# Matmuls of zeros in TensorE's idle stretches, and a phi softmax by halves of the heads

## The chip, the cores and the metric

The kernel runs on one core of a Trainium2 chip. A core has TensorE (PE) for matmuls, VectorE (DVE), ScalarE (ACT) and GpSimd (POOL) for work on vectors, and SyncE (SP), whose queue issues the DMA transfers. The metric is the device time of one execution in microseconds (us).

## The reference

Per batch `b` and head `h` (8 of each, 576 tokens, 64 features), a softmax over 576 tokens of `phi` (32 memories) pools keys and values; queries attend to the pooled memories; the result goes through a real part of a 2D FFT, a layer norm and a feed-forward block (512 to 2048 to 512).

```python
a = exp(phi - max(phi, axis=2)); a = a / (sum(a, axis=2) + 1e-9)
k_m = einsum('bhsm,bhsd->bhmd', a, k); v_m = einsum('bhsm,bhsd->bhmd', a, v)
attn = softmax(scale * q @ k_m.T)          # over the 32 memories
x = (attn @ v_m).transpose(0, 2, 1, 3).reshape(B, S, H * D)
u = x + real(fft(fft(x, axis=1), axis=2))
un = (u - mean(u)) / sqrt(var(u) + 1e-6)
out = u + relu(un @ w_ch1) @ w_ch2
```

## The kernel before

Heads go in four pairs `g`; both heads of a pair fill 128 partitions. The mixing of a batch, `background()`, is a generator that the feed-forward loop advances, so that mixing of later batches runs beside the feed-forward of earlier ones. For batch 0 there is nothing beside it: this is the head of the program.

- `pooling_weights(b)` transposes phi on PE with an f32 identity (`pf`, and its last 64 tokens in `pl`), takes maxima on DVE, exponentials on ACT. For the batches below `NX = 2` it scales the exponentials on ACT (L311), transposes them back (`pt_e`), and copies them to `et`. Each of the two halves holds two head pairs (`g // 2`).
- `pair_memory` multiplies keys and values with `et` in f32: 10 matmuls with 64 columns for each pair, `pm`, which the trace shows as 20 records. DVE masks them with `mk`, a table that a DMA loads (`kmf`, `vmf`).
- `pair_scores` computes 6 matmuls `psc` (12 records) and a softmax of them, mostly on DVE for batch 0 (L440 to L480).
- `values` (`pv`, the transposes `pt_vbd`), `spectrum` (`pa`), `pair_transpose` (`attnT`) and the tiles of `mix_m` and `mix_x` (`pp_t`, `px_t`) give the sums `u` in `uring`. `norm_chunk` normalizes (L631 to L642) and transposes (`pt_unT`).
- The first chunk of the feed-forward block runs in f32: `ffn1_direct` (`ph`, L675) and `ffn2_direct` (`po`, L692). Meanwhile the weights, 64-bit words in memory, are converted to f32 by ACT (L771) and DVE (L773, L774, L784), and split into two f16 parts (L803 to L808). Later chunks use the f16 parts (`ph` L255, `po` L728).

The program is written in sequence, and a scheduler then sets the order of each engine's queue by a timeline of its own; `tc.issue_after` ties single instructions to others. Each engine takes its instructions in the order of its queue.

Of the kernel before, what the change touches and what calls it, by code (L numbers as in the profile page):

```python
# [10 lines left out]
F32 = mybir.dt.float32  # L11
F16 = mybir.dt.float16
# [39 lines left out]
EB = 14  # L52
# [79 lines left out]
def kernel(  # L132
# [10 lines left out]
    nc = tc.nc  # L143

    const = ctx.enter_context(tc.tile_pool(name="const", bufs=1))
    psg = ctx.enter_context(tc.tile_pool(name="psg", bufs=4, space=PSUM))
    ps1 = ctx.enter_context(tc.tile_pool(name="ps1", bufs=2, space=PSUM))
    ps2 = ctx.enter_context(tc.tile_pool(name="ps2", bufs=2, space=PSUM))
# [3 lines left out]
    phs = const.tile([P, NST, NG, 2 * M], F32, name="phs")  # L152
# [15 lines left out]
    mk = small[:, 0:68]  # L168
# [4 lines left out]
    ic = small[:, 714:715]  # L173
    s1, is1, s2, is2 = (small[:, 716 + i * NW : 716 + (i + 1) * NW] for i in range(4))
    ident = small[:, 768:832].bitcast(F16)
    make_identity(nc, ident)
    identf = const.tile([P, P], F32, name="identf")
    make_identity(nc, identf)
    stg = const.tile([P, 3, 4 * UW], F16, name="stg")
    w1t = const.tile([P, NW + 1, 2, NK, UB * P], F16, name="w1t")  # L180
    w2s = const.tile([P, NF + UB, 2, DM], F16, name="w2s")
    nc.gpsimd.memset(ones, 1.0)
    nc.gpsimd.memset(et.rearrange("p g l t c -> p (g l t c)"), 0.0)
    unring = const.tile([P, 2, 2, CH, NK, P], F16, name="unring")
    uring = const.tile([P, NU, DM], F32, name="uring")
    hring = const.tile([P, NW, 2, 4, P], F16, name="hring")

    nk = 2 * NST * P
# [11 lines left out]
    def tiny(tag, n, bufs=2):  # L200
        if tag not in rings:
            rings[tag] = [taken[0], 0]
            taken[0] += n * bufs
        o, i = rings[tag]
        rings[tag][1] += 1
        o += i % bufs * n
        assert taken[0] <= 400, taken
        return scratch[:, o : o + n]
# [6 lines left out]
        return pt[:, c0 : c0 + n]  # L215

    qi = [0]

    def norm_scale(dst_s, dst_i, sq, n, expo, key):

        t = tiny("p2t", 4, 4)
        nc.vector.tensor_scalar(
            out=t[:, :n].bitcast(I32),
            in0=sq.bitcast(I32),
            scalar1=24,
            scalar2=23,
            op0=ALU.logical_shift_right,
            op1=ALU.logical_shift_left,
        )
        nc.vector.tensor_scalar(  # L230
            out=dst_i, in0=t[:, :n], scalar1=2.0**-104, scalar2=2.0 ** (64 - expo), op0=ALU.max, op1=ALU.mult
        )
        nc.vector.reciprocal(out=dst_s, in_=dst_i)

    def transpose(dst, src, on_pe, key):

# [12 lines left out]
    def groups():  # L249

        last = [None]

        def mm(out, lhsT, rhs, start, stop):
            with tc.issue_after(last[0].ins) if start and last[0] is not None else nullcontext():
                m = nc.tensor.matmul(out, lhsT=lhsT, rhs=rhs, start=start, stop=stop)  # L255
            if stop:
                last[0] = m

        return mm


    def load_phi(b):
        for g in range(NG):
            nc.sync.dma_start(out=phs[:, :, g], in_=raw[b, g, :, KV:KVP].rearrange("p (t c) -> p t c", t=NST))

    def load_pair(b, g):
        r = rawt
        if b == 0 and g > 1:
            r = w2s.rearrange("p a l c -> p (a l c)").bitcast(F32)[:, RKQ * (g - 2) : RKQ * (g - 1)]
        elif g % 2 == 1:  # L270
            r = stg[:, 0].bitcast(F32)
        for part, src in ((r[:, :KV], raw[b, g, :, :KV]), (r[:, KV:], raw[b, g, :, KVP:])):
            with tc.issue_after(marks["q"].ins) if b == 0 and "q" in marks else nullcontext():
                marks["q"] = nc.sync.dma_start(out=part, in_=src)
        return r

    def load_vt():
# [2 lines left out]
        marks["vt"] = nc.sync.dma_start(out=v, in_=vt_d)  # L280
        return [v[:, g * 2 * DM : (g + 1) * 2 * DM] for g in range(NG)]

    def pooling_weights(b):

        pl = psg.tile([P, 512], F32, tag="g", name=f"pl_{b}")
        mx = tiny("mx", 4, 2)
        pf = []
        for g in range(2):
            pf.append(psg.tile([P, 512], F32, tag="g", name=f"pf_{b}_{g}"))
            for t in range(NST):  # L290
                dst = pf[g][:, t * P : (t + 1) * P] if t < 4 else pl[:, g * P : (g + 1) * P]
                nc.tensor.transpose(dst, phs[:, t, 2 * g : 2 * g + 2].rearrange("p g c -> p (g c)"), identf)
            nc.vector.tensor_reduce(out=mx[:, g : g + 1], in_=pf[g], axis=AX.X, op=ALU.max)
        rest = pl[:, : 2 * P].rearrange("p (g s) -> p g s", g=2)[:, :, : S - 4 * P]
        nc.vector.tensor_reduce(out=mx[:, 2:4], in_=rest, axis=AX.X, op=ALU.max)
        nc.vector.tensor_tensor(out=mx[:, 0:2], in0=mx[:, 0:2], in1=mx[:, 2:4], op=ALU.max)
        nc.vector.tensor_scalar(out=mx[:, 0:2], in0=mx[:, 0:2], scalar1=-1.0, scalar2=None, op0=ALU.mult)
        su = tiny("su", 4, 2)
        for g in range(2):
            m = mx[:, g : g + 1]  # L300
            nc.scalar.activation(pht[:, g, : 4 * P], pf[g], AF.Exp, bias=m, accum_out=su[:, g : g + 1])
            nc.scalar.activation(pht[:, g, 4 * P :], rest[:, g], AF.Exp, bias=m, accum_out=su[:, 2 + g : 3 + g])
        nc.vector.tensor_tensor(out=su[:, 0:2], in0=su[:, 0:2], in1=su[:, 2:4], op=ALU.add)
        nc.vector.tensor_scalar(
            out=su[:, 0:2], in0=su[:, 0:2], scalar1=1e-9, scalar2=2.0**-EB, op0=ALU.add, op1=ALU.mult
        )
        nc.vector.reciprocal(out=su[:, 2:4], in_=su[:, 0:2])
        for g in range(2):
            r = su[:, 2 + g : 3 + g]
            if b < NX:  # L310
                nc.scalar.activation(pht[:, g], pht[:, g], AF.Copy, scale=r)  # L311
                pt = psg.tile([P, 512], F32, tag="g", name=f"pt_e{b}_{g}")
                for t in range(4):
                    nc.tensor.transpose(pt[:, t * P : (t + 1) * P], pht[:, g, t * P : (t + 1) * P], identf)
                nc.vector.tensor_copy(out=et32[:, g, :4], in_=pt.rearrange("p (t c) -> p t c", c=P))
                half_t = pl[0 : S - 4 * P, (2 + g) * P : (3 + g) * P]
                nc.tensor.transpose(half_t, pht[:, g, 4 * P :], identf)
                nc.scalar.copy(out=et32[0 : S - 4 * P, g, 4], in_=half_t)
                continue
            nc.scalar.activation(elt[:, 0, :S], pht[:, g], AF.Copy, scale=r)  # L320
            nc.vector.scalar_tensor_tensor(
                out=elt[:, 1, :S], in0=pht[:, g], scalar=r, in1=elt[:, 0, :S], op0=ALU.mult, op1=ALU.subtract
            )
            transpose(
                et[:, g].rearrange("p l t c -> p (l t) c"), elt.rearrange("p l c -> p (l c)"), False, f"et_{b}_{g}"
            )
# [319 lines left out]
    def norm_chunk(c):  # L646

        unT = unring[:, c % 2]
        unT0 = unT.rearrange("p l t k c -> p (l t k c)").bitcast(F32)
        unT0 = unT0.rearrange("p (k t c) -> p k t c", k=NK, t=CH)  # L650
        for i in range(CH):
            idx = CH * c + i
            norm_tile(idx, us[idx], un[:, i])
            if c == 0:
                pt = psg.tile([P, 512], F32, tag="g", name=f"pt_unT_{i}")
                for k in range(NK):
                    nc.tensor.transpose(pt[:, k * P : (k + 1) * P], un[:, i, k * P : (k + 1) * P], identf)
                marks["uh0"] = nc.scalar.copy(out=unT0[:, :, i], in_=pt.rearrange("p (k c) -> p k c", k=NK))
        if c == 0:
            return unT0  # L660
        marks[f"uh{c}"] = nc.scalar.copy(out=ud[:, 0], in_=un)  # L661
        marks[f"ul{c}"] = nc.gpsimd.tensor_tensor(out=ud[:, 1], in0=un, in1=ud[:, 0], op=ALU.subtract)  # L662
        transpose(
            unT.rearrange("p l t k c -> p (l t k) c"), ud.rearrange("p l t c -> p (l t c)"), False, f"unT_{c}"
        )
        return unT
# [181 lines left out]
    marks = {}  # L848
# [6 lines left out]
    def background():  # L855
# [56 lines left out]
        while True:  # L912
            yield n_tiles, 0

    load_phi(0)
    first = [load_pair(0, 0)]
    nc.sync.dma_start(out=mk, in_=mk_d)
    first += [load_pair(0, g) for g in range(1, NG)]
    marks["load"] = marks["q"]
    with tc.issue_after(marks["load"].ins):  # L920
# [29 lines left out]

    while made < 2:
        made, room = next(bg)
    unTs = {0: norm_chunk(0)}
    hs = {c: [] for c in range(n_chunks)}
    po = [ps2.tile([P, 512], F32, tag="o", name=f"po_0_{t}") for t in range(CH)]
# [29 lines left out]
    for n in range(NW, n_steps):  # L985
        c, j = divmod(n, NW)
# [75 lines left out]
```

## Time and profile before

| | us |
|---|---|
| median of 3 runs | 996.77 (996.4 to 997.15) |
| the profiled execution | 996.51 |
| its span | 994.6 |
| PE busy | 955.8 (96% of the span) |
| DVE busy | 568.1 (57%) |
| ACT busy | 456.3 (46%) |
| POOL busy | 228.0 (23%) |

The span goes from the first to the last instruction; 1.9 us of the time lie around it. PE's busy time counts from the start of a matmul to its modelled end, so it does not tell whether the array streams all the time. The page also has a row of the clock that was granted to PE, in tenths of full speed, in 40 slices of 24.9 us. The profile's lines below have, if they are single instructions: start, length, engine, line, operation, tile written <- tiles read, shape, count, and in brackets the idle time before and what ended it.

### The profile page before, as it was taken

How to read it: one execution, taken by the hardware profiler on the slowest of the kernel's cores; microseconds unless marked ns; L12 is line 12 of the kernel's file. 1: busy time of each engine (PE TensorE's matmuls, PEld its weight loads, DVE VectorE, ACT ScalarE, POOL GpSimd, SP SyncE). 2: the span in 40 equal slices, each digit the busy share in tenths (PEclk: the TensorE clock that was granted, in tenths of full speed). 3: DMA queues.
4: the chain of work that ended last, by engine and by line, in shares of the span. 5: the costliest groups of instructions: out<-in, count | busy, mean ns of one | idle time of the engine just before them, and what ended most of it. 6: DMA issues, size and time to landing. Idle time of an engine off the chain costs nothing.

```text
span 994.6 us, 18638 instructions
## 1 busy us (share of the span) xinstructions
PE 955.8 (96%) x7644; PEld 685.8 (69%) x7644; DVE 568.1 (57%) x1287; ACT 456.3 (46%) x913; POOL 228.0 (23%) x249
## 2 busy tenths in 40 slices
PE   5769999899999999999999999999999999999998
PEld 5756678666677777767767767777777777766664
DVE  1689967867655575657532576657745676311111
ACT  2265557586535563655431555456545543411100
POOL 1122235235221241233120032113311241300000
PEclk9979999999999999999999999999999999999999
DMA  9706545064222641384210643164213411210000
GB/s 351 270 1 253 184 152 154 2 138 117 64 43 59 136 98 41 56 153 103 58 22 22 117 120 61 48 119 121 68 43 62 101 19 35 44 39 4 22 22 22
DMA packets 115957, 88.06 MB, mean 89 GB/s; under 512 B 100384, under 2 KB 100384, under 8 KB 113824
## 3 DMA queue, kind: packets, MB, share of 16 engines
q1 hardware_dynamic: 115872, 86.87, 34.6%
q8 instruction: 60, 0.98, 0.4%
q14 instruction: 25, 0.20, 0.1%
HBM read 58.15 MB, written 9.44 MB: 68 GB/s over the span
## 4 chain that ended last, share of the span: by engine, by line
PE 84%; DVE 9%; ACT 2%; DMA 2%; issue 1%; SPq 0%; POOL 0%; DVEq 0%; ACTq 0%; POOLq 0%
PE po L728 34%; PE ph L255 33%; PE pm L255 5%; PE pp_t L255 3%; PE psc L255 2%; PE px_t L255 1%; PE pa L548 1%; PE pv L521 1%; PE po L692 1%; DVE w1t L784 1%; DVE uring L617 1%; DVE w2s L774 1%; DMA et<-elt 1%; DMA uring<-in_w 1%; DMA rawt<-in_raw 1%
## 5 line engine op out<-in xcount | busy, mean ns | idle before, releaser
L255 PE MATMUL ph<-unring,w1t 128*128 128x256 f16 x3264 | 390.3, 273 | 2.4 <-DVE scratch L638 1.4
L728 PE MATMUL po<-w2s,hring 128*128 128x512 f16 x1632 | 381.1, 380 | 3.1 <-ACT w2s L838 1.8
L255 PEld LDWEIGHTS <-w1t 128*128 128x128 f16 x3264 | 316.0, 98 | 66.3 <-issue 2.6
L728 PEld LDWEIGHTS <-hring 128*128 128x128 f16 x1632 | 157.6, 98 | 161.5 <-issue 5.6
L719 DVE SCALAR_TENSOR_TENSOR hring<-ph,hring 128x512 f16<-128x512 f32 x136 | 93.3, 686 | 157.4 <-ACT hring L718 156.9
L718 ACT ACTIVATE hring<-ph 128x512 f16<-128x512 f32 x136 | 80.1, 589 | 167.7 <-PE ph L255 167.6
L456 POOL TENSOR_TENSOR aring<-aring,scratch 128x384 f32<-128x384 f32 x28 | 24.7, 882 | 186.6 <-DVE scratch L454 163.5
L641 POOL TENSOR_TENSOR scratch<-scratch,small 128x1 f32<-128x1 f32 x36 | 23.9, 679 | 165.6 <-DVE scratch L640 152.9
L255 PEld LDWEIGHTS <-stg 128*128 128x128 f16 x1152 | 46.1, 98 | 10.3 <-issue 1.7
L373 POOL TENSOR_TENSOR stg<-rawt,stg 128x640 f16<-128x640 f32 x12 | 17.6, 1464 | 122.4 <-ACT rawt L372 122.4
L662 POOL TENSOR_TENSOR ud<-un,ud 128x1024 f16<-128x1024 f32 x17 | 36.7, 2160 | 33.9 <-ACT ud L661 33.8
L255 PE MATMUL pm<-et,stg 128*128 128x64 f16 (+1 forms) x780 | 39.1, 203 | 2.0 <-DMA et<-elt 2.0
L440 DVE TENSOR_REDUCE scratch<-psc 128x12 f32<-128x384 f32 x32 | 17.8, 556 | 39.2 <-PE psc L255 39.1
L255 PE MATMUL pp_t<-vh,at 128*128 128x255 f16 (+3 forms) x288 | 36.7, 273 | 0.0
L603 DVE SCALAR_TENSOR_TENSOR share<-pp_t,scratch,small 128x257 f32<-128x257 f32 (+1 forms) x48 | 21.0, 479 | 26.6 <-ACT small L600 26.5
L740 DVE SCALAR_TENSOR_TENSOR uring<-po,small,uring 128x512 f32<-128x512 f32 x34 | 24.5, 744 | 19.2 <-PE po L728 19.2
L675 PE MATMUL ph<-unring,w1t 128*128 128x256 f32 x128 | 33.5, 409 | 2.0 <-DVE w1t L784 1.5
L475 ACT CAST aeo<-eo 128x384 f16<-128x384 f32 x30 | 15.3, 510 | 43.9 <-DVE eo L472 43.9
L450 ACT ACTIVATE aring<-aring,scratch 128x384 f32<-128x384 f32 x24 | 14.6, 610 | 45.0 <-DVE aring L449 45.0
L617 DVE SCALAR_TENSOR_TENSOR uring<-px_t,scratch,share 128x256 f32<-128x256 f32 (+1 forms) x80 | 33.9, 476 | 0.2
L692 PE MATMUL po<-w2s,hring 128*128 128x512 f32 x64 | 31.5, 621 | 2.4 <-ACT hring L678 2.4
L675 PEld LDWEIGHTS ph<-unring,w1t 128*128 128x128 f32 x128 | 26.0, 207 | 11.1 <-issue 4.6
(226 smaller groups left out, 1271.9 us busy)
## 6 DMA issues: line engine op xcount, KB each, us to landing
rawt<-in_raw SPq DMA_DIRECT2D x15, 640.0 KB, 5.6
stg<-in_raw SPq DMA_DIRECT2D x15, 640.0 KB, 5.1
out<-uring SPq DMA_DIRECT2D x36, 256.0 KB, 2.1
stg<-in_w SPq DMA_DIRECT2D x7, 1024.0 KB, 5.1
rawt<-in_raw SPq DMA_DIRECT2D x15, 384.0 KB, 3.2
stg<-in_raw SPq DMA_DIRECT2D x15, 384.0 KB, 3.2
phs<-in_raw SPq DMA_DIRECT2D x32, 160.0 KB, 5.2
w2s<-in_w SPq DMA_DIRECT2D x4, 1024.0 KB, 9.6
```

The source lines that it names most:

```text
L255: m = nc.tensor.matmul(out, lhsT=lhsT, rhs=rhs, start=start, stop=stop)
L456: eng.tensor_tensor(out=a, in0=a, in1=sm.unsqueeze(2).to_broadcast([P, 12, M]), op=ALU.mult)
L603: nc.vector.scalar_tensor_tensor(out=tm[rows, w * NJ : (w + 1) * NJ], in0=pp[rows, :NJ], scalar=beta[rows], in1=qs[rows], op0=ALU.mult, op ...
L617: nc.vector.scalar_tensor_tensor(out=u[rows, hs], in0=px[rows, hs], scalar=igx[rows], in1=tm[rows, w * NJ + half : w * NJ + half + 256], o ...
L641: nc.gpsimd.tensor_tensor(out=rs, in0=rs, in1=half, op=ALU.pow)
L662: marks[f"ul{c}"] = nc.gpsimd.tensor_tensor(out=ud[:, 1], in0=un, in1=ud[:, 0], op=ALU.subtract)
L675: nc.tensor.matmul(ph, lhsT=w[:, k, f * P : (f + 1) * P], rhs=unTs[0][:, k], start=(k == 0), stop=(k == NK - 1))
L692: nc.tensor.matmul(po[t], lhsT=h[:, f, t], rhs=w[:, f], start=(j == 0 and f == 0), stop=(j == NW - 1 and f == UB - 1),)
L718: nc.scalar.activation(h[:, 0], phv, AF.Relu)
L719: nc.vector.scalar_tensor_tensor(out=h[:, 1], in0=phv, scalar=0.0, in1=h[:, 0], op0=ALU.max, op1=ALU.subtract)
L728: nc.tensor.matmul(po[t], lhsT=hs[j][:, lh, f * 2 + t], rhs=w2s[:, j * UB + f, lw, :], start=(j == 0 and f == 0 and i == 0), stop=(j == NW ...
L740: nc.vector.scalar_tensor_tensor(out=u, in0=po[t], scalar=cout if c else 0.5, in1=u, op0=ALU.mult, op1=ALU.add)
```

## The change

1. `keep_busy(n)` issues `n` f16 matmuls 128x128 by 128x512 of zeros into a PSUM buffer of the pool `ps2` that nothing reads. The zeros lie in the last slot of `uring`, which DVE clears at the start. `KEEP` has the numbers: 8 ahead of phi, 18 behind phi's transposes, 4 and 3 behind the transposes back of the two halves, 22 ahead of the first norm. `marks["pe"]` ties them behind the matmul that was issued last.
2. For the batches below `NX`, `pooling_f32` replaces the common softmax: maximum, sum and reciprocal are taken for each half by itself, and DVE instead of ACT scales the exponentials (128x576, in place).
3. A small Exp of a single column at the start makes ACT load its table there; the f32 identity is built before the f16 one.
4. The load of `mk` is written ahead of all others.

```diff
+KEEP = [8, 18, 0, 0, 22, 4, 3]
...
-    make_identity(nc, ident)
+    uring = const.tile([P, NU, DM], F32, name="uring")
+    zeros = uring[:, NU - 1].bitcast(F16)[:, :DM]
+    nc.vector.memset(zeros, 0.0)
     identf = const.tile([P, P], F32, name="identf")
     make_identity(nc, identf)
+    make_identity(nc, ident)
+    warm = const.tile([P, 1], F32, name="warm")
+    nc.vector.memset(warm, 0.0)
+    nc.scalar.activation(warm, warm, AF.Exp)
...
+    def keep_busy(n):
+
+        pt = ps2.tile([P, 512], F32, tag="o", name=f"keep_{len(kept)}")
+        kept.append(pt)
+        with tc.issue_after(marks["pe"].ins) if "pe" in marks else nullcontext():
+            for _ in range(n):
+                nc.tensor.matmul(pt, lhsT=zeros[:, :P], rhs=zeros, start=True, stop=True)
...
+    def pooling_f32(b, pl, pf, rest):
+
+        mx, su = tiny("mx", 4, 2), tiny("su", 4, 2)
+        for g in range(2):
+            nc.vector.tensor_reduce(out=mx[:, g : g + 1], in_=pf[g], axis=AX.X, op=ALU.max)
+            nc.vector.tensor_reduce(out=mx[:, 2 + g : 3 + g], in_=rest[:, g], axis=AX.X, op=ALU.max)
+            m = mx[:, g : g + 1]
+            nc.vector.tensor_scalar(
+                out=m, in0=m, scalar1=mx[:, 2 + g : 3 + g], scalar2=-1.0, op0=ALU.max, op1=ALU.mult
+            )
+            nc.scalar.activation(pht[:, g, : 4 * P], pf[g], AF.Exp, bias=m, accum_out=su[:, g : g + 1])
+            nc.scalar.activation(pht[:, g, 4 * P :], rest[:, g], AF.Exp, bias=m, accum_out=su[:, 2 + g : 3 + g])
+        if b == 0:
+            keep_busy(KEEP[1])
+        for g in range(2):
+            t = su[:, g : g + 1]
+            nc.vector.tensor_scalar(
+                out=t, in0=t, scalar1=su[:, 2 + g : 3 + g], scalar2=1e-9, op0=ALU.add, op1=ALU.add
+            )
+            nc.vector.tensor_scalar(out=t, in0=t, scalar1=2.0**-EB, scalar2=None, op0=ALU.mult)
+            nc.vector.reciprocal(out=t, in_=t)
+            nc.vector.tensor_scalar(out=pht[:, g], in0=pht[:, g], scalar1=t, scalar2=None, op0=ALU.mult)
+        for g in range(2):
...
+            marks["pe"] = nc.tensor.transpose(half_t, pht[:, g, 4 * P :], identf)
+            if b == 0:
+                keep_busy(KEEP[5 + g])
+            nc.vector.tensor_copy(out=et32[:, g, :4], in_=pt.rearrange("p (t c) -> p t c", c=P))
+            nc.scalar.copy(out=et32[0 : S - 4 * P, g, 4], in_=half_t)
...
-            if b < NX:
-                nc.scalar.activation(pht[:, g], pht[:, g], AF.Copy, scale=r)
...
+    nc.sync.dma_start(out=mk, in_=mk_d)
     load_phi(0)
+    keep_busy(KEEP[0])
     first = [load_pair(0, 0)]
-    nc.sync.dma_start(out=mk, in_=mk_d)
...
     while made < 2:
         made, room = next(bg)
+    keep_busy(KEEP[4])
     unTs = {0: norm_chunk(0)}
```

PE's queue between the transposes of phi and the first `pm`, before; `pl` takes the last 64 tokens of both directions:

```order
L292 MATMUL pf_1_135<-identf,phs 128x128 x4
L292 MATMUL pl_127<-identf,phs 128x128
L314 MATMUL pt_e_0_153<-identf,phs 128x128 x4
L317 MATMUL pl_127<-identf,phs 64x128
L314 MATMUL pt_e_1_162<-identf,phs 128x128 x4
L255 MATMUL pm_0_170<-et,rawt 128x64 x10
```

The same place now:

```order
L340 MATMUL pf_1_147<-identf,phs 128x128 x4
L340 MATMUL pl_140<-identf,phs 128x128
L248 LDWEIGHTS uring
L248 MATMUL keep_163<-uring 128x512
L323 MATMUL pt_e_0_190<-identf,phs 128x128 x4
L325 MATMUL pl_140<-identf,phs 64x128
L323 MATMUL pt_e_1_203<-identf,phs 128x128 x4
L270 MATMUL pm_0_215<-et,rawt 128x64 x10
```

The pair of `keep` stands here 18 times, and further ones behind both `pl` of the transposes back (4 and 3).

DVE's queue from the last masking of `pm` to the first sums of the scores' softmax, before; the conversion of the first weights stands between the second and the third pair:

```order
L347 TENSOR_TENSOR vmf<-pm_1_183,small 128x128
L773 TENSOR_SCALAR w1t<-w1t 128x1024
L774 SCALAR_TENSOR_TENSOR w1t<-w1t 128x1024
L784 SCALAR_TENSOR_TENSOR w1t<-w1t 128x1024
L346 TENSOR_TENSOR share<-pm_2_196,small 128x64
L347 TENSOR_TENSOR vmf<-pm_2_196,small 128x128
L346 TENSOR_TENSOR share<-pm_3_209,small 128x64
L347 TENSOR_TENSOR vmf<-pm_3_209,small 128x128
L440 TENSOR_REDUCE scratch<-psc_0_222 128x12
```

Now, at the scores:

```order
L389 TENSOR_TENSOR vmf<-pm_3_254,small 128x128
L815 TENSOR_SCALAR w1t<-w1t 128x1024
L482 TENSOR_REDUCE scratch<-psc_0_267 128x12
L816 SCALAR_TENSOR_TENSOR w1t<-w1t 128x1024
L491 TENSOR_TENSOR aring<-psc_0_267,scratch 128x384
L482 TENSOR_REDUCE scratch<-psc_1_291 128x12
L826 SCALAR_TENSOR_TENSOR w1t<-w1t 128x1024
```

The three operations of the conversion moved from among the `pm` to among the scores.

SP's queue from the last load of a head pair on, before; `small` holds the masks, `hring` takes the table `vt`:

```order
L274 DMA w2s<-in_raw 128x768
L922 DMA ct<-in_ct 128x1740
L761 DMA w1t<-in_w 128x2048
L917 DMA small<-in_mk 128x68
L280 DMA hring<-in_vt 128x4096
```

The same place now:

```order
L289 DMA w2s<-in_raw 128x768
L965 DMA ct<-in_ct 128x1740
L957 DMA small<-in_mk 128x68
L803 DMA w1t<-in_w 128x2048
L295 DMA hring<-in_vt 128x4096
```

The load of the masks, written first, stands behind phi, the pairs and `ct`; it moved past the first weights only. Behind the head the order of many instructions differs on every engine.

More of the change, by code (lines that the diff above doesn't have):

```diff
@@ L184 @@
     unring = const.tile([P, 2, 2, CH, NK, P], F16, name="unring")
-    uring = const.tile([P, NU, DM], F32, name="uring")
     hring = const.tile([P, NW, 2, 4, P], F16, name="hring")
@@ L217 @@
     qi = [0]
+    kept = []
     def norm_scale(dst_s, dst_i, sq, n, expo, key):
@@ L256, in mm @@
             if stop:
-                last[0] = m
+                last[0] = marks["pe"] = m
         return mm
@@ L281, in load_vt @@
         return [v[:, g * 2 * DM : (g + 1) * 2 * DM] for g in range(NG)]
+    def pooling_f32(b, pl, pf, rest):
[20 more added lines that the diff above has]
+        for g in range(2):
+            pt = psg.tile([P, 512], F32, tag="g", name=f"pt_e{b}_{g}")
+            for t in range(4):
+                nc.tensor.transpose(pt[:, t * P : (t + 1) * P], pht[:, g, t * P : (t + 1) * P], identf)
+            half_t = pl[0 : S - 4 * P, (2 + g) * P : (3 + g) * P]
+            marks["pe"] = nc.tensor.transpose(half_t, pht[:, g, 4 * P :], identf)
[3 more added lines that the diff above has]
+            nc.scalar.copy(out=et32[0 : S - 4 * P, g, 4], in_=half_t)
     def pooling_weights(b):
@@ L291, in pooling_weights @@
                 dst = pf[g][:, t * P : (t + 1) * P] if t < 4 else pl[:, g * P : (g + 1) * P]
-                nc.tensor.transpose(dst, phs[:, t, 2 * g : 2 * g + 2].rearrange("p g c -> p (g c)"), identf)
-            nc.vector.tensor_reduce(out=mx[:, g : g + 1], in_=pf[g], axis=AX.X, op=ALU.max)
+                marks["pe"] = nc.tensor.transpose(dst, phs[:, t, 2 * g : 2 * g + 2].rearrange("p g c -> p (g c)"), identf)
+            if b >= NX:
+                nc.vector.tensor_reduce(out=mx[:, g : g + 1], in_=pf[g], axis=AX.X, op=ALU.max)
         rest = pl[:, : 2 * P].rearrange("p (g s) -> p g s", g=2)[:, :, : S - 4 * P]
+        if b < NX:
+            pooling_f32(b, pl, pf, rest)
+            return
         nc.vector.tensor_reduce(out=mx[:, 2:4], in_=rest, axis=AX.X, op=ALU.max)
@@ L309, in pooling_weights @@
             r = su[:, 2 + g : 3 + g]
-            if b < NX:
-                nc.scalar.activation(pht[:, g], pht[:, g], AF.Copy, scale=r)
[L312 to L319, printed above, removed]
             nc.scalar.activation(elt[:, 0, :S], pht[:, g], AF.Copy, scale=r)
```

## The prediction

> **What bounds the kernel now.** I read the share of the engines first, then the chain that ended last in order of time, then the busy time and clock by stretches, then single instructions of the head.
>
> ```profile
> span 994.6 us, 18638 instructions
> PEclk9979999999999999999999999999999999999999
> 0.00:75.00 75.00, 51.28 (x274) 45.67 (x275) 42.56 (x105) 29.41 (x54) 14.54 (x24) 0.93 0.56 206
> 75.00:200.00 125.00, 115.77 (x739) 87.01 (x738) 104.50 (x231) 73.02 (x141) 38.53 (x33) 0.97 0.47 150
> 200.00:994.50 794.50, 788.71 (x6635) 553.16 (x6633) 421.03 (x953) 353.85 (x720) 174.89 (x192) 1.00 0.31 68
> ```
>
> After the stretch's length the columns of the last three lines are PE, weight loads, VectorE (DVE), ScalarE (ACT), GpSimd (POOL), granted clock, DMA share, GB/s. Behind 200 us TensorE (PE) is idle for 5.8 us in all, between 75 and 200 for 9.2, but in the first 75 us for 23.7. So from 75 us on the time is PE work that the change keeps; only the head can move, and a shift of its end should move the end of the program. The chain tells what the head is made of (start, length, what):
>
> ```profile
> 7.23 0.69 DVE scratch L293
> 9.88 0.78 ACT phs L301 x2
> 10.65 0.30 ACT phs L302 x2
> 13.43 1.12 PE pt_e L314 x4
> 15.83 16.96 PE pm L255 x80
> 32.79 5.13 PE psc L255 x24
> 138.98 1.28 PE psc L255 x12
> 148.92 2.23 PE pm L255 x20
> ```
>
> The 80 `pm` records of batch 0 take 16.96 us, 0.212 each. In batch 1 the same shape takes 2.23 for 20, 0.112 each; `psc` goes from 5.13/24 = 0.214 to 1.28/12 = 0.107. The head's PE runs at half speed, though the clock row begins with 9: that row is to be believed only where a change is recorded. Around the changes it reads:
>
> ```profile
> 69.33:72.74 3.41, 3.41 (x10) 2.69 (x9) 3.38 (x4) 3.41 (x4) 1.77 (x1) 0.50 0.00 0
> 93.22:96.63 3.41, 1.48 (x10) 0.96 (x9) 3.41 (x9) 1.69 (x4) 0.33 (x1) 1.00 0.98 413
> 96.63:100.04 3.41, 3.41 (x7) 1.68 (x6) 3.41 (x8) 1.19 (x1) 3.41 (x2) 0.50 0.77 264
> 100.04:103.45 3.41, 3.41 (x13) 2.26 (x12) 3.41 (x9) 3.30 (x6) 0.52 (x1) 1.00 0.00 0
> 147.83:151.25 3.42, 3.42 (x33) 3.42 (x32) 2.73 (x7) 0.68 (x2) 0.67 (x1) 1.00 0.67 150
> 195.62:199.04 3.42, 3.35 (x8) 1.16 (x8) 3.42 (x8) 2.29 (x6) 2.10 (x1) 0.50 0.02 5
> ```
>
> Every change of clock falls on a grid of 3.41 us. After a stretch that is full of wide matmuls (69.33 to 72.74, 96.63 to 100.04) the clock goes up; after one with 1.48 us of PE work (93.22) it goes down. The stretch from 147.83 holds 20 `pm` and 8 `psc` records and keeps the full clock. Cold, the same kind of work ran from 15.83 to 37.9 without raising it: 64 streamed columns behind each 128-column weight load, so PE is "busy" while half of its streaming time is empty. So `pm` can hold the clock but not raise it.
>
> **The sum, part by part.** It is made against the profiled execution: 996.51 us, span 994.6; the median of the runs, 996.77, is 0.03% above it.
>
> *Start of `pm`, +0.5 (-1.2 to +2.2).* The rows for the data:
>
> ```profile
> 6.10 1.09 PE L292 MATMUL pf<-identf,phs 128*128 128x128 f32 x4 [0.55 <-DMA phs<-in_raw]
> 8.58 1.28 ACT L301
> 99.98 0.53 DVE L642 TENSOR_SCALAR un<-uring,scratch 128x512 f32<-128x512 f32 x1
> 14.66 0.69 DVE L315 COPY et<-pt_e 128x512 f32<-128x512 f32 x1 [2.15 <-PE pt_e L314]
> 103.89 0.60 PE L292 MATMUL pf<-identf,phs 128*128 128x128 f32 x4
> 195.69 6.55 PE L728 MATMUL po<-w2s,hring 128*128 128x512 f16 x22 [1.33 <-DVE w2s L843]
> ```
>
> L301 at 8.58 is the load of ACT's table; it moves under the wait for phi. After the last maximum at 7.92 come a short reduce and a scale (0.4), the exponentials of one half with their sums (0.78 + 0.30), four DVE operations on one column (0.7) and one DVE scaling of 576 columns, 0.53 to 0.66 by the 512-column row: the first half could be transposed at about 10.7 instead of 13.43. But 18 zero matmuls stand ahead of it in PE's queue. A 128x512 f16 matmul takes 3.35/8 = 0.42 at half clock (stretch from 195.62) and, in the 6.55 us after that, about 0.216 at full clock. From the last phi transpose (7.2): if the 8 matmuls ahead of phi have already raised the clock, the 18 end at 11.1; else the first full stretch of the grid closes between 10.6 and 14.0 and the rest runs warm, so they end between 12.8 and 14.5. I take 12.8, the middle of 11.1 and 14.5, because the grid's phase against the program is not fixed by anything in the trace. From there: transposes 0.60, copy 0.69, scaling of the second half 0.6 (it stands behind that copy on DVE), transposes 0.6, three zero matmuls 0.65: `pm` starts at 16.0 instead of 15.6, with 14.4 and 17.8 as ends. The first 8 zero matmuls (3.4 cold, from about 0.8) end near 4.2; the f32 identity, now built first, is ready by then, but neither helps nor hurts, since the second half of phi's transposes waits for its DMA until 6.10. Zeroing, the small Exp and the masks' load fall on engines that have nothing else to do yet. The four zeros behind the first transposes (0.86) lie under copy and scaling. If that cover went they would cost 0.86.
>
> *`pm` and the first `psc` warm, -9.3.* 16.96 - 4 x 2.23 = 8.04, and 5.13/2 - 1.28 = 1.29. The first `psc` releases DVE, so VectorE's chain starts that much earlier. The table of masks is used first after `pm_0`:
>
> ```profile
> 21.06 0.23 DVE L346 TENSOR_TENSOR share<-pm,small 128x64 f32<-128x64 f32 x1 [4.71 <-DMA small<-in_mk]
> ```
>
> It landed at 21 and would now hold up `pm_0`'s reader, which is ready near 18.4. In SP's queue it moves past one weight load only, about 2.5 us of DMA (1 MB at 413 GB/s, stretch from 93.22), so it lands near 18.5: nothing is held. The weight load behind it is later by 34 KB, below 0.1 us.
>
> *DVE's chain, +1.9 (+1.2 to +3.1).*
>
> ```profile
> 35.39:55.12 19.73, 13.22 (x72) 10.69 (x71) 18.80 (x56) 9.03 (x20) 6.69 (x8) 1.00 0.40 127
> 24.63 0.68 DVE L773 TENSOR_SCALAR w1t<-w1t 128x1024 int32<-128x1024 int32 x1
> 25.35 1.23 DVE L774 SCALAR_TENSOR_TENSOR w1t<-w1t 128x1024 int32<-128x1024 int32 x1
> 26.61 1.22 DVE L784 SCALAR_TENSOR_TENSOR w1t<-w1t 128x1024 uint32<-128x1024 uint32 x1
> 37.12 0.55 DVE L452 TENSOR_REDUCE scratch<-aring 128x12 f32<-128x384 f32 x1 [0.59 <-ACT aring L450]
> ```
>
> From the first scores at 35.39 to 55.12 DVE is busy 18.80 of 19.73: it is the bound. The conversion of the first weights (0.68, 1.23, 1.22) lay under cold `pm`; now the first stands ahead of the scores (under `psc_0`), the other two among them: +2.45. They fill the wait of 0.59: +1.9. Ends: another half microsecond of such waits filled, or all 3.13 added.
>
> *Spectrum, +1.0 (0 to +2).* After `psc` PE waits for DVE for several us, so the clock falls. Before, a run of `pv`, `pa` and transposes raised it between the two `pa` rows below (0.94 for six, then 0.55), in time for the `pp_t` and `px_t` of the first tiles; now `pv` and the four `pa` lie apart.
>
> ```profile
> 50.48 0.94 PE L548 MATMUL pa<-ct,aeo 128*128 128x145 f16 x6
> 54.26 0.55 PE L548 MATMUL pa<-ct,aeo 128*128 128x145 f16 x6
> 76.39 1.48 PE L255 MATMUL pp_t<-vh,at 128*128 128x257 f16 x12
> 58.63 1.34 PE L255 MATMUL px_t<-vbdt,attnT 128*128 128x128 f16 x16
> ```
>
> Cold, 12 `pp_t` (1.48 us warm) and 16 `px_t` (1.34) take up to twice as long, some of it beside ACT and DVE.
>
> *The 22 zeros ahead of the norm, 0 (0 to +1); warm transposes, -0.8.*
>
> ```profile
> 65.26 1.94 PE L657 MATMUL pt_unT<-identf,un 128*128 128x128 f32 x8 [5.29 <-DVE un L642]
> 67.72 1.12 ACT L771 ACTIVATE w2s<-w2s 128x1024 f32<-128x1024 f32 x1
> 73.95 0.36 ACT L678 ACTIVATE hring<-ph 128x256 f32<-128x256 f32 x1
> ```
>
> They take 22 x 0.216 = 4.75 inside a wait of 5.3; with one cold stretch of 3.41 (8 of them) 6.4, +1. The eight transposes behind them then take 1.1 (from 0.60 for four) instead of 1.94: -0.8. The warm `ph` matmuls bring nothing more: the first activation of `ph` waits for six ACT passes from 67.72 to 73.95.
>
> *Batch 1, +0.4 (0 to +1.3).* Its softmax scaling moves from ACT to DVE, 2 x 0.53 to 0.66, in a stretch where DVE is nearly full; DVE waits of 0.85 and 0.98 us take some:
>
> ```profile
> 118.85 0.70 DVE L779 TENSOR_SCALAR stg<-stg 128x1024 uint32<-128x1024 uint32 x1 [0.85 <-DMA stg<-in_w]
> 122.60 0.43 DVE L773 TENSOR_SCALAR w1t<-w1t 128x512 int32<-128x512 int32 x1 [0.98 <-ACT w1t L771]
> ```
>
> Sum: 0.5 - 9.3 + 1.9 + 1.0 + 0 - 0.8 + 0.4 = -6.3, so **990.2 us**. All good ends: -10.1, 986.4. All bad ends, without the warm transposes: +0.3, 996.8.
>
> **Rivals.** *1, slower: zeros do not count.* If a matmul of zeros does not raise the clock, nothing does: the 18 end at 14.8 (0.42 each), the transposes, 4 zeros, transposes, 3 zeros put `pm` at about 19.9 (+4.3), still cold; DVE's chain pays +1.9; 22 of 0.42 are 9.2 in a gap of 5.3 (+3.9); with batch 1 +10.5, 1007 us. It decides at the first `pm`: 0.21 apart, not 0.11. No matmul of zeros is in this trace; for the forecast speaks that narrow and wide work of equal busy time were treated differently, so what is measured looks like streamed columns, not a share of time.
>
> *2, no change: the clock is raised but lost in `pm`.* 3.41 us warm are 30 `pm`, the other 50 cold 10.7, `psc_0` 2.57: 16.7 against 10.2, so 6.5 of the gain goes, 996.7. Against it stands the stretch from 147.83 at 1.00; for it, that this is a single grid stretch, while here `pm` and `psc` last three to four. The Trainium skill (TensorE: Matmul & The Clock Gate, "A second HAM failure mode: psum-queue depth-cycling") says that short idles between groups of matmuls can make the clock oscillate, which would be this rival. The same page's Part 1 has the clock fall only after an idle window; by that, `pm` stays warm and the sum stays 990.2. The trace disagrees with it as stated: 93.22 to 96.63 had 1.48 us of PE work and the clock still fell.
>
> *3, given back behind the head.* The instructions behind 75 us are put in another order on all engines, and DVE is 84% busy from 75 to 200 (104.50 of 125). If PE's 9.2 us of waits there grow by 4, the time is 994 to 997.
>
> **Chances.** Forecast 0.70; rival 1 0.08; rival 2 0.10; rival 3 0.09; else 0.03. A measurement of this kernel can tell about 0.2%, 2 us. Faster by more: 0.66 from the forecast, 0.06 from rival 3 and the rest, 0.72. Within 0.2%: the forecast's bad end, rivals 2 and 3, 0.14. Slower: rival 1 and the bad ends of 2 and 3, 0.14. The range goes from 985.5 (the good ends, and a little for the new order) to 997.5, which takes in rivals 2 and 3 and leaves out rival 1 and the edges.
>
> **What the changed profile would show.** `pm` records 0.112 apart and 80 of them in about 9 us from 16; DVE's first reduction of scores near 26.5 instead of 35.4; two conversions between the reductions of scores; the first unT transposes near 59 and eight in 1.1; no clock of 0.50 there; PE's waits from 75 us on of the same size. The prediction is wrong if `pm` stays 0.21 apart, if the 18 or the 22 zeros end later than the data, or if PE's waits behind the head grow.

## The result, and the profile after

| | before | after |
|---|---|---|
| median of 3 runs, us | 996.77 | 987.98 (986.68 to 988.82) |
| the profiled execution | 996.51 | 987.98 |
| its span | 994.6 | 986.2 |

The ratio is 0.991, interval 0.9888 to 0.9933: faster by 8.8 us. Run once more it was 0.9926 (0.9901 to 0.9951). The three executions of the kernel before all belong to the longer of two groups into which its executions fall (see "What the gain is made of"); against the mean of 101 more of them, 994.4, the mean of the changed kernel's nine, 988.3, is 6.1 us lower. The page of the profile after, its span and clock row, and the busy time by stretches (columns as in the prediction):

```profile
span 986.2 us, 18761 instructions
PEclk9699999999999999999999999999999999999999
0.00:75.00 75.00, 58.77 (x376) 42.07 (x377) 51.47 (x122) 31.72 (x60) 15.16 (x25) 0.86 0.62 228
75.00:200.00 125.00, 116.85 (x732) 85.39 (x730) 99.39 (x236) 76.71 (x144) 38.60 (x34) 0.97 0.46 139
200.00:986.00 786.00, 781.82 (x6595) 550.05 (x6593) 416.80 (x945) 345.69 (x708) 171.41 (x191) 1.00 0.30 68
```

From 75 us on PE's idle time is as before (8.2 and 4.2 us, before 9.2 and 5.8). The gain is in the head, though the clock row got worse (0.86, before 0.93): ahead of the first recorded change the row says 1.00, whatever the clock was. The chain of the head (start, length, what):

```profile
6.90 3.88 PE keep L248 x18
10.78 0.44 PE pt_e L323 x4
13.91 8.88 PE pm L270 x80
22.79 1.35 PE psc L270 x12
24.64 1.22 DVE w1t L816
26.70 1.22 DVE w1t L826
```

80 `pm` take 8.88 us, 0.111 each, against 16.96 before. The same stretch on the grid of the clock, whose changes fell at 4.87, 32.17, 49.24, 66.31 and 69.72, each a multiple of 3.41 from the others:

```profile
1.46:4.87 3.41, 3.41 (x9) 1.17 (x8) 0.00 (x0) 0.76 (x2) 3.06 (x6) 1.00 0.97 202
4.87:32.17 27.30, 22.67 (x175) 19.11 (x174) 15.48 (x47) 7.47 (x20) 0.00 (x0) 1.00 1.00 401
32.17:49.24 17.07, 10.48 (x70) 7.12 (x71) 13.56 (x41) 8.93 (x18) 6.58 (x8) 0.50 0.68 224
49.24:66.31 17.07, 13.25 (x79) 8.76 (x78) 13.45 (x26) 10.94 (x16) 3.90 (x3) 1.00 0.00 0
```

The stretch from 1.46, full of zeros but for the first transposes of phi, opened the clock at 4.87 (its own 1.00 is the unrecorded cold); it then held through all of `pm` and `psc`. Single instructions at the ends of the head's parts, after, and of before the one that the prediction does not show:

```profile
24.17 0.56 DVE L482 TENSOR_REDUCE scratch<-psc 128x12 f32<-128x384 f32 x1 [0.32 <-PE psc L270]
51.33 4.91 PE L248 MATMUL keep<-uring 128*128 128x512 f16 x22
56.61 1.25 PE L699 MATMUL pt_unT<-identf,un 128*128 128x128 f32 x8 [0.37 <-DVE un L684]
65.14 5.37 PE L734 MATMUL po<-w2s,hring 128*128 128x512 f32 x8 [2.89 <-ACT hring L720]
```
```profile
74.45 1.96 PE L692 MATMUL po<-w2s,hring 128*128 128x512 f32 x4 [0.47 <-ACT hring L678]
```

The first `po` comes 9.3 us earlier (74.45 to 65.14), the end of the span 8.4. So 0.9 us of the head's gain went behind it.

### The profile page after: what moved, and what is told of

It reads as the page before. It is cut to its first block, busy times and chain, and to the rows that moved or that the text cites. A ratio compares the mean times of both kernels' runs of the same rounds, so it can differ in the third digit from the quotient of the medians.

```text
span 986.2 us, 18761 instructions
## 1 busy us (share of the span) xinstructions
PE 957.5 (97%) x7699; PEld 677.5 (69%) x7699; DVE 567.7 (58%) x1301; ACT 454.1 (46%) x910; POOL 225.2 (23%) x249
## 4 chain that ended last, share of the span: by engine, by line
PE 84%; DVE 9%; DMA 3%; issue 2%; ACT 2%; POOL 0%; SPq 0%; DVEq 0%; ACTq 0%; POOLq 0%
PE po L770 35%; PE ph L270 34%; PE pm L270 4%; PE pp_t L270 3%; PE psc L270 2%; PE px_t L270 1%; PE pa L590 1%; PE pv L563 1%; DVE w2s L816 1%; PE po L734 1%; DVE w1t L826 1%; DVE w1t L816 1%; PE pf L340 1%; DVE w1t L850 1%; DMA rawt<-in_raw 1%
## 5 line engine op out<-in xcount | busy, mean ns | idle before, releaser
L734 PE MATMUL po<-w2s,hring 128*128 128x512 f32 x64 | 35.2, 688 | 4.9 <-ACT hring L720 2.9
L270 PE MATMUL pm<-et,stg 128*128 128x64 f16 (+1 forms) x780 | 37.1, 199 | 0.5 <-DMA et<-elt 0.5
L782 DVE SCALAR_TENSOR_TENSOR uring<-po,small,uring 128x512 f32<-128x512 f32 x34 | 24.5, 743 | 19.5 <-PE po L770 19.5
L508 POOL TENSOR_TENSOR aring<-aring 128x128 f32<-128x128 f32 x56 | 31.4, 582 | 2.2
L270 PEld LDWEIGHTS <-at 128*128 128x128 f16 (+1 forms) x288 | 28.5, 102 | 4.4 <-issue 1.8
```

The costliest lines, as they stand in the source:

```text
L508: eng.tensor_tensor(out=a2[:, i : i + 4], in0=a[:, 0:4], in1=a[:, 4:8], op=op)
L734: nc.tensor.matmul(po[t], lhsT=h[:, f, t], rhs=w[:, f], start=(j == 0 and f == 0), stop=(j == NW - 1 and f == UB - 1),)
L782: nc.vector.scalar_tensor_tensor(out=u, in0=po[t], scalar=cout if c else 0.5, in1=u, op0=ALU.mult, op1=ALU.add)
```

## The experiments

The changed kernel once more and eleven variants of it, each executed 6 to 12 times; the range stands behind each median. The kernel before, executed beside them, had medians of 995.7 to 996.4. Starts of instructions are those of PE's timeline, in the one execution of each kernel that was profiled; there `pm` starts at 13.75 in the changed kernel and the first `po` at 65.14.

**The change once more.** 

> The changed kernel once more, beside the others on one chip. Theory (the zeros open the clock early, the clock holds through pm): 988 us, 8.8 below the kernel before; the first clock change again between 4 and 14 us, on another phase of the 3.41 us grid, and the start of pm between 13.9 and 17.8 with it, so single runs differ by up to 3 us. Rival (the gain is a lucky phase): runs that open the clock late are near 992 or more.

988.48 (986.74 to 991.09). In the profiled execution the clock opened at 5.54 and `pm` started at 14.22, inside the expected range. The six executions differ by 4.4 us, more than the expected 3.

**No zeros.** `KEEP = [0, 0, 0, 0, 0, 0, 0]`; everything else of the change stays.

> No matmul of zeros at all; softmax by halves, early table load and order of loads kept. Theory: pm runs cold, 0.21 us apart; its start moves from 15.8 to about 14.3 by the softmax alone, so 995.3 us (1.5 below before), little else. Rival (the softmax and the new order carry the gain): 988 to 990.

994.12 (986.8 to 1000.08; ratio 0.9985, 0.9956 to 1.0013), near the expected 995.3. Ten of the twelve executions took 993.8 or more; two took 986.8 and 988.65, as some of the kernel before do. PE's timeline:

```profile
13.26 4.37 PE L272 MATMUL pm<-et,rawt 128*128 128x64 f32 x20
30.22 2.77 PE L272 MATMUL psc<-share,rawt 128*128 128x64 f32 x12
```

`pm` starts earlier than in the changed kernel but runs 0.21 apart to the end: the first recorded change of clock is at 52.58. The first `po` comes at 72.19, before at 74.45, in the changed kernel at 65.14. So in the head 7.0 us come from the zeros and 2.3 from the softmax by halves and the rest; by the times alone the latter cannot be told from nothing.

**The common softmax, with zeros.**

```diff
-            if b >= NX:
+            if True:
...
-        if b < NX:
-            pooling_f32(b, pl, pf, rest)
-            return
...
+        if b == 0:
+            keep_busy(KEEP[1])
...
+                nc.scalar.activation(pht[:, g], pht[:, g], AF.Copy, scale=r)
```

The scaling of the exponentials goes back to ACT with it; the early load of ACT's table stays.

> All zeros kept, but the common softmax of the kernel before for the first batches (scaling on ACT), with the early table load. Theory: pm warm, started about 1.1 later than in the changed kernel (15.0 instead of 13.9), so 989 us; the DVE scaling in batch 1 goes, up to 0.4 back. Rival (the halves matter as much as the clock): 992 or more.

991.13 (990.27 to 993.57), 2 worse than expected. `pm` starts at 14.49, warm, and the first `po` at 65.76, 0.6 later than with the halves (for `pm` 1.1 was expected). The other 1.9 us came behind the first `po`, where the order is another: between 150 and 200 us PE is idle for 9.7 us, in the changed kernel for 4.6.

**Without the first 8, and with 7 alone.** `KEEP = [0, 18, 0, 0, 22, 4, 3]`:

> Without the 8 zeros ahead of phi. Theory: the 18 behind phi must open the clock themselves; the first full stretch of the grid closes between 10.6 and 14.0, so they end between 12.8 and 14.5 and pm starts 2 to 3.7 later than 13.9; pm is warm; 990 to 992 us. Rival (the transposes of phi, or part of a stretch, are enough): 988.

988.47 (986.49 to 989.08), below the expected 990 to 992. The clock opened at 9.56, earlier than expected:

```profile
6.15:9.56 3.41, 3.01 (x10) 1.82 (x11) 1.30 (x4) 0.73 (x3) 0.00 (x0) 1.00 1.00 387
```

This stretch had 3.01 us of PE work, transposes of phi and then zeros, with idle time at its start, so a stretch need not be full to open the clock. The first `po` came at 66.39, 1.25 later; 0.6 of it was left at the end of the span (986.7 against 986.2). Then `KEEP = [0, 0, 0, 0, 22, 4, 3]`:

> The changed kernel with the 8 and the 18 zeros left out; the 4 and 3 behind the transposes back and the 22 ahead of the norm stay. Theory (one stretch of the grid of 3.41 us that is nearly full opens the clock): transposes back, 4 zeros, transposes, 3 zeros fill PE without a gap for about 5.2 us from 10.4 (0.6 x 2 cold, 4 x 0.42, 1.2, 3 x 0.42), so a stretch at least 0.8 full lies in it in about 9 of 10 positions of the grid; the clock opens between 13.8 and 17.2, pm starts near 15.5 and runs at 0.11 apart from then on, the head ends 2 to 3 us later than with all zeros: 988 to 991. Rival (it takes the long run of zeros, more than one full stretch): pm stays 0.21 apart, 994 as with no zeros at all.

987.88 (986.46 to 989.65, 12 runs): as fast as with all zeros. PE's timeline, and two stretches of its grid:

```profile
12.56 1.91 PE L250 MATMUL keep<-uring 128*128 128x512 f16 x4
14.27 1.06 PE L325 MATMUL pt_e<-identf,phs 128*128 128x128 f32 x4
15.33 1.18 PE L250 MATMUL keep<-uring 128*128 128x512 f16 x3
16.35 2.34 PE L272 MATMUL pm<-et,rawt 128*128 128x64 f32 x20
9.24:12.65 3.41, 1.19 (x6) 1.12 (x7) 2.13 (x10) 1.82 (x8) 0.00 (x0) 1.00 1.00 405
12.66:16.07 3.41, 3.41 (x12) 1.85 (x11) 1.42 (x3) 0.52 (x2) 0.00 (x0) 1.00 1.03 419
```

One full stretch, made of 4 zeros, transposes and most of the 3 zeros, opened the clock at 16.07, within the expected 13.8 to 17.2. The head ended 1.7 us later than in the changed kernel (`po` at 66.86), and this execution took 989.65, the longest of the twelve and 1.7 above the profiled one of the changed kernel. All twelve lie below the 994 of the rival.

**Narrow zeros.** 64 columns instead of 512, in four times as many matmuls:

```diff
-            for _ in range(n):
-                nc.tensor.matmul(pt, lhsT=zeros[:, :P], rhs=zeros, start=True, stop=True)
+            for _ in range(4 * n):
+                nc.tensor.matmul(pt[:, :64], lhsT=zeros[:, :P], rhs=zeros[:, :64], start=True, stop=True)
```

> Every matmul of zeros with 512 columns becomes four with 64 columns, each with its own 128-column weight load: the same busy time at half clock (4 x 0.107 for 0.427 us), but half of the streaming time empty, as in pm. Theory (streamed columns open the clock, not busy time): it stays at half, the 72 narrow ones end near 14.6, pm starts near 18 and runs 0.21 apart, the 88 ahead of the norm take 9.4 us in a wait of 5.3: 1003 to 1008 us. Rival (any busy time opens it): 988 to 990.

993.48 (990.94 to 994.97): neither the theory nor the rival. The premise fell: I took it that each 64-column matmul of zeros would pay for its weight load, as `pm` does, and leave half of the stream empty. Timeline and stretches:

```profile
7.43 4.05 PE L248 MATMUL keep<-uring 128*128 128x64 f16 x72
54.61 2.73 PE L248 MATMUL keep<-uring 128*128 128x64 f16 x88
5.55:8.96 3.41, 2.63 (x34) 2.59 (x35) 1.54 (x4) 0.35 (x1) 0.00 (x0) 1.00 0.97 368
8.97:12.38 3.41, 3.41 (x52) 3.32 (x50) 1.75 (x9) 1.79 (x8) 0.00 (x0) 1.00 1.02 409
56.75:60.17 3.42, 0.94 (x24) 0.85 (x20) 2.75 (x9) 0.00 (x0) 1.17 (x2) 1.00 0.00 0
```

A narrow f16 matmul took 0.056 cold and 0.031 warm; an eighth of the wide one's 0.216 is 0.027. So the stream stays nearly full, and it opened the clock at 12.38, after the first full stretch; the one before it, with 2.63 us of work, did not. Four 64-column matmuls stream half of the columns of one wide one, so the zeros filled less time: 88 ahead of the norm were over at 57.3, the stretch from 56.75 had 0.94 us of work, the clock fell, and `po` came at 68.78. The rest went behind the head, where PE waited 5.0 us instead of 2.0 for the `w2s` of POOL that the next experiment is about. Whether streamed columns or busy time open the clock was not told apart here.

**Without the 22 ahead of the norm.** `KEEP = [8, 18, 0, 0, 0, 4, 3]`:

> Without the 22 zeros ahead of the first norm. Theory: the clock falls in the wait, the eight unT transposes take 1.9 instead of 1.25 us, and all behind them is 0.7 later; the matmuls of the first ph are slow again but hidden behind ACT: 989 us, no difference that can be told from the changed kernel. Rival (the cold ph and po behind the norm lie on the path): 991 or more.

995.92 (994.57 to 998.19, 12 runs), no faster than before. The head explains only 1.4 us of it: `po` starts at 66.57, and 0.7 of the 1.4 is the cold clock at the norm (9.19 us from `unT` to `po` instead of 8.53). PE, POOL and DVE in their timelines, without the 22 zeros:

```profile
112.32 3.44 PE L736 MATMUL po<-w2s,hring 128*128 128x512 f32 x4 [10.35 <-POOL w2s L826]
96.81 12.12 POOL L706 TENSOR_TENSOR ud<-un,ud 128x1024 f16<-128x1024 f32 x1 [4.04 <-ACT ud L705]
108.89 3.37 POOL L826 TENSOR_TENSOR w2s<-w2s 128x1024 int32<-128x1024 int32 x1
105.74 1.21 DVE L818 SCALAR_TENSOR_TENSOR w1t<-stg,w1t 128x1024 int32<-128x1024 int32 x1
107.06 2.96 DVE L828 SCALAR_TENSOR_TENSOR w1t<-stg,w1t 128x1024 uint32<-128x1024 uint32 x1
```

and in the changed kernel:

```profile
105.90 5.40 PE L734 MATMUL po<-w2s,hring 128*128 128x512 f32 x8 [2.00 <-POOL w2s L824]
97.50 2.13 POOL L704 TENSOR_TENSOR ud<-un,ud 128x1024 f16<-128x1024 f32 x1 [3.31 <-ACT ud L703]
103.12 2.73 POOL L824 TENSOR_TENSOR w2s<-w2s 128x1024 int32<-128x1024 int32 x1 [3.48 <-DVE w2s L816]
97.73 2.98 DVE L850 SCALAR_TENSOR_TENSOR w1t<-w1t,small 128x1024 f16<-128x1024 f32 x1
```

POOL's `ud` takes 2.13 us or 12.12. In the second case DVE runs instruction behind instruction without a pause from 96.9 on, and POOL seems to get through only at about 107, where DVE's own operation is stretched from 1.2 to 2.96; in the first POOL got through at once and DVE's L850 took 2.98 (1.27 without POOL beside it). By these lengths one engine waits for the other, at times DVE and at times POOL. The `w2s` that PE needs stands behind `ud` in POOL's queue. The order on DVE there differs between the two kernels, since the scheduler counts the zeros in its timeline.

The Trainium skill (SBUF — State Buffer, "Who interferes with whom") says that a DVE instruction with two SBUF inputs contends with a GpSimd instruction that reads SBUF, and that the ports they share are an exclusive lock. The lengths here agree with an exclusion, but POOL's operation was held up for 10 us, through a whole row of DVE instructions of at most 1.3 us each, not for one.

**The same, with POOL's operations moved to DVE.** First `ud`; the 22 zeros stay out:

```diff
-        marks[f"ul{c}"] = nc.gpsimd.tensor_tensor(out=ud[:, 1], in0=un, in1=ud[:, 0], op=ALU.subtract)
+        marks[f"ul{c}"] = (nc.vector if c == 1 else nc.gpsimd).tensor_tensor(out=ud[:, 1], in0=un, in1=ud[:, 0], op=ALU.subtract)
```

> The kernel without the 22 zeros, in which one more operation is moved: the low f16 part of the second chunk (ud, 128x1024), which took POOL 12.12 us there (2.13 in the changed kernel), goes to DVE; nothing else changes its place on any queue near it. Theory A (what that kernel lost is POOL's wait for DVE at this operation, and PE's wait of 10.35 us for the w2s that POOL had queued behind it): DVE pays about 1.3, PE's wait at 102 us falls to 1 to 4, 987 to 990. Theory B (what it lost is the cold clock at the norm, 57 to 64 us): 995 to 997, as without this edit.

991.83 (990.47 to 993.54, 12 runs): 4.1 better, between the two theories.

```profile
110.16 5.82 PE L736 MATMUL po<-w2s,hring 128*128 128x512 f32 x8 [8.38 <-POOL w2s L826]
101.21 8.89 POOL L826 TENSOR_TENSOR w2s<-w2s 128x1024 int32<-128x1024 int32 x1 [8.67 <-issue]
107.96 3.23 DVE L828 SCALAR_TENSOR_TENSOR w1t<-stg,w1t 128x1024 uint32<-128x1024 uint32 x1
```

The wait went to the next operation of POOL: `w2s` started at 101.21 and, with DVE's row unbroken until 107.8, took 8.89 instead of 2.73. Then this one too:

```diff
-LP = ["2_0", "2_2", "2_4", "2_6"]
+LP = ["2_0", "2_2", "2_6"]
```

> The kernel without the 22 zeros, with ud's low part on DVE (991.83 us, PE waits 8.38 us for POOL's w2s, which took 8.89 there) and now also the last step of that w2s on DVE (1.21 in place of the shift's 0.67), so that POOL has no long operation between 92 and 117 us. Theory A (what is lost is POOL's wait for DVE, at whichever of its operations meets DVE's unbroken row): PE's wait for w2s at 102 us falls below 3, DVE's 3.23 us operation at 108 returns to 1.2, and the time to 986 to 989. Theory B (the rest of the loss is the cold clock at the norm, and POOL's wait only shows where PE had to wait anyway, for DVE): PE waits as long for DVE's w2s, 991 to 993.

992.5 (990.4 to 993.98, 12 runs). Theory A was right on the wait and wrong on the time. PE's timeline of this kernel, and then the busy time in two stretches, of the kernel without the 22 zeros, of this one, and of the changed one:

```profile
106.62 3.72 PE L719 MATMUL ph<-unring,w1t 128*128 128x256 f32 x16 [2.28 <-DVE w1t L828]
110.18 7.03 PE L736 MATMUL po<-w2s,hring 128*128 128x512 f32 x16
```
```profile
75.00:150.00 75.00, 63.79 (x301) 44.83 (x300) 59.42 (x112) 35.02 (x64) 30.22 (x12) 0.93 0.54 185
150.00:200.00 50.00, 44.96 (x392) 36.30 (x392) 39.45 (x120) 34.79 (x71) 18.18 (x21) 0.94 0.36 80
```
```profile
75.00:150.00 75.00, 71.19 (x371) 52.00 (x370) 62.64 (x131) 39.38 (x71) 16.57 (x14) 1.00 0.63 213
150.00:200.00 50.00, 40.28 (x347) 31.15 (x347) 37.65 (x109) 35.40 (x71) 16.00 (x18) 0.98 0.25 57
```
```profile
75.00:150.00 75.00, 71.43 (x352) 50.94 (x350) 61.33 (x127) 40.17 (x73) 22.53 (x17) 0.95 0.61 196
150.00:200.00 50.00, 45.42 (x383) 34.45 (x381) 38.07 (x109) 36.53 (x72) 16.07 (x18) 0.99 0.22 54
```

Ahead of 150 us PE no longer waits for POOL, and DVE's L828 is back at 1.22. The 7.4 us that PE lost before 150 are back (63.79 to 71.19), and 4.7 of them are idle again behind it (44.96 to 40.28): besides a wait of 3.1 for a DMA, which the changed kernel has too (3.0), PE waits there for DVE and POOL, 1.9, 1.6, 1.2 and 1.2, where the changed kernel has no wait above 0.5. The head was also 1.8 us later in the profiled execution, because the clock opened at 10.62 only. That PE's wait came from the stretched operations of POOL is shown; that its removal alone gives the time back is not. Which order behind 150 us would keep the gain stays open.

**Zeros in more gaps, and the conversion later.** 14 zeros behind `as_vq`, 14 behind `pv`, 12 between the halves of the spectrum:

> The changed kernel with 14, 14 and 12 more zeros in PE's waits behind as_vq, behind pv and between the two halves of the spectrum, so that the clock does not fall at 32 us. Theory: pa, the attnT transposes and pp_t ahead of the first tiles run warm; of their cold time about 0.8 us lies on the path: 987.2 us. Rival (it is hidden, or the zeros come in the way of pv and pa): 988 to 990.

987.21 (984.81 to 988.16). The number is the expected one and cannot be told from the change's; the reason is not the expected one, so the hit is luck. The clock now stays open to 41.41, but the first transposes `unT` start at 57.58 instead of 56.61 and `po` at 66.05, 0.9 later than in the changed kernel, since DVE sets the time there and the zeros stand ahead of the real work. What was gained came behind the head. The conversion of the first weights gated behind the last scores:

```diff
-GATE1 = [[]] + [["un1", "uh0"]] * 7
+GATE1 = [["a0_3"]] + [["un1", "uh0"]] * 7
```

> The changed kernel with the conversion of the first weights tied behind the last scores of batch 0 (the copy of the fourth pair's aeo on ACT). Theory (the conversion costs DVE's chain 1.2 to 2.4 us where the change put it): the spectrum's last pa starts 2 us earlier than 44.9; the conversion then stands beside the attnT copies; 986 to 987 us. Rival (its cost only moves to the attnT and norm steps): 988.

986.19 (984.54 to 988.25), in the expected range, but not for the expected reason: the second half of the spectrum starts at 44.78, 0.16 earlier, the first `po` at 65.43, later than in the changed kernel. PE is busy for 73.89 of 75 us between 75 and 150, 2.5 more than there; the gain is in the order behind the head. Both together:

> Zeros in further gaps (14 behind as_vq, 14 behind pv, 12 between the spectrum's halves) and the conversion of the first weights behind pair 3's scores, together. Apart they gave 987.2 and 986.2. If their gains add: 985.4. If the gaps' zeros only fill waits that the conversion made: 986.2. If the new order meets a wait like the 10.35 us of the kernel without the 22 zeros: 992 or more.

992.02 (990.45 to 993.13). The gains do not add: the zeros behind `pv` now start late (from 40.06; the `pa` behind them starts at 44.43), the spectrum's second half comes at 48.04, 3.1 later than in the changed kernel, and `po` at 67.48. The version with the late conversion alone is the fastest found, 1.8 us below the change; but its ratio to before, 0.9915 (0.9886 to 0.9944), takes in the change's, so the two cannot be told apart.

## Why the prediction was right, and where it was not

Forecast 990.2 in 985.5 to 997.5, measured 987.98. By the steps (in brackets the starts or lengths before and after, from the rows shown, `pm` by the chain; the last step ends with the spans):

| step | predicted | measured |
|---|---|---|
| start of `pm` | +0.5 | -1.9 (15.83 to 13.91) |
| `pm` and first `psc` warm, to DVE's first reduction | -9.3 | -9.3 (19.56 to 10.26) |
| from there to `unT`: DVE's chain, spectrum, 22 zeros | +2.9 | +2.6 (29.87 to 32.44) |
| `unT` to the first `po` | -0.8 | -0.7 (9.19 to 8.53) |
| behind the first `po` | +0.4 | +0.9 (920.2 to 921.1) |

- *Start of `pm`.* This term was mis-sized by 2.4 us, and it makes up the miss of 2.2; the other terms miss by up to 0.9 each, and these misses nearly cancel, which is luck. The step that failed is the middle between 11.1 and 14.5 for the end of the 18 zeros: the 8 ahead of phi had already opened the clock, so the 18 took 3.88 and ended at 10.78, the good end. The middle gave both cases the same weight. Of the nine profiled executions here with these 8 wide zeros, eight opened the clock between 3.86 and 6.76; one, the kernel with both of POOL's operations moved, opened it at 10.62, and there `pm` started at 16.27. So the good end is the usual case. Without the 8 the clock opened at 9.56 and `pm` started at 15.08, both earlier than the sum's assumption of a stretch that has to be full.
- *Rival 1 (zeros do not count)* fell with the first `pm` at 0.11, *rival 2 (lost in `pm`)* with 0.111 over all 80.
- *`pm` can hold the clock but not raise it*: the run without zeros agrees, and all 80 `pm` and the `psc` behind them ran warm in the changed kernel. The hold has a limit, though: in batch 1 of the changed kernel the clock fell at 124.33, after a stretch whose 3.03 us of PE work were 20 `pm` and a few small matmuls:

```profile
120.92:124.33 3.41, 3.03 (x26) 2.95 (x26) 3.29 (x7) 1.31 (x3) 0.00 (x0) 1.00 0.12 19
```

  That nothing raises the clock in the old head may be too strong, see below.
- *DVE's chain.* The two conversions of 1.22 stand among the reductions, as told. The second half of the spectrum starts (PE's timeline, after and before)

```profile
44.94 0.42 PE L582 MATMUL pa<-ct,aeo 128*128 128x290 f16 x1 [2.89 <-DVE aeo L522]
```
```profile
55.18 0.30 PE L540 MATMUL pa<-ct,aeo 128*128 128x290 f16 x1 [0.38 <-DVE aeo L480]
```

  20.77 us behind the first reduction, before 19.79: +1.0, not +1.9. And gating the conversion away gained only 0.3 of it: waits for `psc` came in its place. From there to `unT` it was +1.6 (predicted +1.0 for the spectrum).
- *The 22 zeros.* In place they cost nothing, as predicted: they end at 56.24 and PE then still waits 0.37. But I priced them in their gap alone. Without them the time is 996, only 0.7 us of it by the clock at the norm and most because the order of the queues behind changes. That is rival 3, and it was one edit away: all it takes is POOL's `ud` meeting an unbroken row on DVE.
- *Masks.* They landed at 19.5 (I had 18.5). Their reader on DVE waited for them, since `pm` was early, but PE's `pm` went on without a gap.

**What the gain is made of.** Beside the experiments the kernel before ran 101 times: 29 executions took 986.9 to 989.4 us, 72 took 995.3 to 999.8, none lay between. The mean granted clock on record is 0.986 to 0.988 in the 29 and 0.990 to 0.997 in the 72; the changed kernel has 0.982 to 0.987. Since an unrecorded cold start counts as 1.00, the lower figure fits a clock which opens early and falls again in DVE's stretch. So it seems that in 3 of 10 executions the old head opened the clock by itself, where a stretch of the grid happened to begin with the transposes back (`pt_e`, from 13.43) and to hold none of the idle time before them; a clock that was still open at the start would fit as well. No execution of that group was profiled: this is argued, not shown. If it is so, the change does not make the best execution faster, it makes the good one the rule: its nine executions took 986.7 to 991.1. The Trainium skill (TensorE: Matmul & The Clock Gate, "What's actually happening") says that the window of the clock runs freely and does not start anew with the kernel; the traces agree: its first opening in the same kernel was at 4.87 and at 5.54. The 3.4 us of sustained activity that the same page of the Trainium skill asks for do not suffice here, though: 17 us of `pm`, busy all the time, left the clock at half.

## What to carry to other kernels

Ahead of a long run of narrow f32 matmuls, a few wide matmuls of zeros that close the gaps over one stretch of the clock's grid can open the clock for the whole run (here 0.111 us for each `pm` instead of 0.212): 7 did here what 33 did, and zeros in further gaps, where another engine sets the pace, gave nothing that can be told from noise. Dummy work is not free of side effects where a scheduler prices it: after each such edit look for a new wait far behind it, above all where GpSimd has a long operation beside an unbroken row on VectorE. And time the kernel before often enough to see whether its executions fall in groups, since a change may only move executions from one group to the other.

## What the runs showed of the hardware that was not expected

- GpSimd's `ud`, 2.13 us in the changed kernel, took 12.12 beside an unbroken row of VectorE instructions; a `w2s` of 2.73 took 8.89.
- Narrow f16 matmuls (64 columns) showed no price for their weight loads, 0.031 each; f32 ones of the same shape take 0.111.
- A stretch of 3.41 us full of wide or f16 matmuls opened the clock (at 4.87, 12.38, 16.07), but it need not be full. With wide zeros alone 2.67 us of work opened it (at 3.86, in the run with zeros in more gaps) and 2.60 did not (to 3.79, in the run with both of POOL's operations moved); one execution each:

```profile
0.45:3.86 3.41, 2.67 (x7) 1.00 (x8) 0.28 (x2) 1.49 (x2) 3.09 (x7) 1.00 0.54 121
```
```profile
0.38:3.79 3.41, 2.60 (x7) 0.95 (x8) 0.28 (x2) 1.49 (x2) 3.08 (x9) 1.00 0.51 115
```

- Busy time alone does not decide: 3.41 us of 3.41 of narrow f32 matmuls did not open the clock, and the clock fell after 3.03 us that were mostly such work (120.92, in the changed kernel) as well as after 0.94 (56.75).
